# Softmax sums by block transposes from couple 11 on instead of couple 9, half of them moved into the first half of a couple

## The chip, the cores and the metric

The kernel runs on one core of one Trainium2 chip. The metric is the device time of one launch in microseconds (us), the median of some runs. All data are 32-bit floats. The engines are named as the profile names them: PE (matrix products), DVE (vector engine), ACT (activation engine), POOL (GpSimd) and SP (here only a queue of DMAs). PE writes its results to the banks of PSUM, and DVE or ACT must read a bank out (drain it) before PE may fill it again.

## The reference

Attention with normalised queries and keys, and a two-layer network with a SiLU behind it:

```python
# q, k, v: (8 batches, 12 heads, 448 rows, 64); w_in: (768, 2048); w_out: (2048, 768)
rms = np.sqrt(np.mean(x * x, axis=-1, keepdims=True) + 1e-06)     # for x = q and x = k
q_n, k_n = q / rms_q * g_q, k / rms_k * g_k
scores = (1 / np.sqrt(64)) * np.matmul(q_n, k_n.transpose(0, 1, 3, 2))
attn = np.exp(scores - scores.max(-1, keepdims=True))
attn = attn / (attn.sum(-1, keepdims=True) + 1e-09)
x = np.matmul(attn, v)            # then (batch, row, head * 64) -> (3584, 768)
h = x @ w_in
out = (h * (1 / (1 + np.exp(-h)))) @ w_out
```

## The kernel before

**Couples.** The attention is worked off in 24 couples (`c` = 0 to 23), of two pairs of heads each: four heads of one batch. Three couples make a batch, and six (`GROUP`) make two batches, whose network layer is then computed. For a couple, `scores` gives the transposed scores of a block of keys on PE and their exponentials on ACT (L788, with k's norm as ACT's scale), and `weigh` multiplies the exponentials with v on PE (L820, into the banks `av0` and `av1`). `visit(c)` holds these two for couple c, and at its start the end of couple c-1: `divide(c - 1, sums)` (L892) multiplies that couple's result by the inverse softmax sums, which lie in `both_r` (`r[0]` and `r[1]`).

**Between two visits.** `between(c)` runs PE on the first network layer of the last two batches, which is computed by Strassen's seven products (`Seven`): three matmuls of 448 columns each (L992), 14 matmuls in each of the two halves of a `between`. The products go to banks `mm` (two of them) and `sc` (two, which the scores also use). DVE drains most products with an addition (L941), ACT copies some (L1003, L1012) and later applies the SiLU to them (L1145). `fill(others, prompt)` deals other work among these matmuls, in the order in which it is written: `others` evenly over the half, `prompt` one piece at the start and one after each product. What is dealt stands in its engine's queue at that place, and every engine works its queue off in order.

**The other work of a couple.** In the first half: `flip(c + 1, "q")` (L682), `add` (L834), which adds the exponentials of the key blocks up (block 1 in the visit, blocks 2 and the left one, `LEFT`, here), and `normalise(c + 2)`, whose last two pieces are k's sums of squares (ACT squares by L474 into a scratch tile, DVE sums them by L475, POOL takes the root by L503). In the second half, from couple 9 on (`FOLDED = LATE`): `fold(c, i)` twice, which gives the softmax sums over the 128 key rows: DVE transposes 32 x 32 blocks of the added weights into `turned`, a region that holds weights no longer needed (L717), and reduces them (L718). Then `flip(c + 1, "k")` (L686) with ACT's `gain` (L692), and q's squares (L699 on ACT, L705 on DVE). `close(c)` then joins the two halves of rows with small matmuls (L731 for q's norms, L736 for the folded sums) into one `sc` bank, inverts the sums and spreads them by another block transpose (L745, L749, L751); POOL takes q's roots (L743) and scales q (L762).

**Sums on PE.** Couples 6 to 8 get their sums by `sum_up` instead: matmuls of the weights with ones (L861), two reciprocals of 128x224 on DVE (`invert`, L870), a copy (L876) and four DMAs on SP's queue (`spread`, L879), which copy each half of the rows to where the other is. Couple 6 has two such terms (eight matmuls in place of four), because its left block isn't added by DVE.

**Rounding of w_in.** Until couple 10, DVE also rounds and sums w_in (L126, L129, L133; the sums L938 and L941 on `W`).

The order of the instructions on each engine is that in which the program is written; nothing reorders it.

Of the kernel before, what the change touches and what calls it, by code (L numbers as in the profile page):

```python
# [11 lines left out]
F32 = mybir.dt.float32  # L12
# [15 lines left out]
BANK = 512  # L28
# [514 lines left out]
def bounded(  # L543
# [13 lines left out]
    GROUP, LATE = z.NPAIR, z.LATE  # L557
    EARLY = GROUP - 1
    SOON = 2 * GROUP - 1
    FOLDED = LATE  # L560
# [54 lines left out]
    def weights(c, j):  # L615

        return other if j == 0 and c < GROUP and c % 2 else e[j]
# [95 lines left out]

    def fold(c, i):

        turned = weights(c, 1)[:, 1].rearrange("p h s -> p (h s)")
        nc.vector.transpose(turned, weights(c, 0)[:, i].rearrange("p h s -> p (h s)"))  # L717
        nc.vector.tensor_reduce(  # L718
            out=folded[:, ts(i, n)], in_=turned.rearrange("p (n e) -> p n e", e=z.Q),
            axis=AX.X, op=ALU.add,  # L720
        )
# [116 lines left out]
    def sum_up(c):  # L838
# [6 lines left out]
        if c < GROUP:  # L845
            t = bank(S)
        else:
            t = ps.tile([P, 2, BANK], F32, name="sc", bufs=2)[:, 0, 0:S]
# [3 lines left out]
        if c == GROUP:  # L852
            terms.insert(0, (1, None))
# [42 lines left out]
    def normalise(c):  # L896


        def piece(name, i):
            t = scratch[i if c < GROUP + 2 else 0]  # L900
# [612 lines left out]
    def visit(c):  # L1513
# [23 lines left out]
        if c > 0:  # L1537
# [12 lines left out]
            else:  # L1550
                divide(c - 1, sums)
# [46 lines left out]
    def between(c):  # L1598

        def transposes_and_sums():  # L1600
            if c >= FOLDED:
                if c < LATE - 1:
                    transpose_k(c + 1)
                turns = [lambda: flip(c + 1, "k"), gain] if LATE - 1 <= c < NC - 1 else []
                return [lambda: fold(c, 0), lambda: fold(c, 1)] + turns
# [53 lines left out]
        late += further[2:] if c >= GROUP else further[:2]  # L1659
# [10 lines left out]
        if c >= LATE - 2:  # L1670
# [4 lines left out]
            steps = weights_in(c, 1)  # L1675
# [22 lines left out]
    begun, inverting = {}, []  # L1698
# [243 lines left out]
```

## Time and profile before

| | |
|---|---|
| median of three runs | 1295.49 us (1294.70 to 1296.91) |
| the profiled execution | 1295.43 us, its span 1293.6 us |
| PE busy | 1274.9 us, 99% of the span |
| DVE busy | 992.7 us, 77% |
| ACT busy | 504.0 us, 39% |
| POOL busy | 361.2 us, 28% |
| mean granted clock of PE | 0.996 |

The first line is what the launch took from outside, the span is what the instructions take from the first to the last, and the difference of the second row, 1.8 us, lies around the program. Busy time counts an engine's work and not its waiting. The attention takes the span's first 708 us, and the rest is the last network group and the second layer. Times below are us from the span's start; in the timeline a row gives start, length, engine, line, operation, output and inputs, and in brackets how long the engine stood idle before it and for whom. In the table by stretches a row gives the stretch, its length, each engine's busy time with its number of instructions, and PE's granted clock (1.00 is full).

### The profile page before, as it was taken

How to read it: one execution, taken by the hardware profiler on the slowest of the kernel's cores; microseconds unless marked ns; L12 is line 12 of the kernel's file. 1: busy time of each engine (PE TensorE's matmuls, PEld its weight loads, DVE VectorE, ACT ScalarE, POOL GpSimd, SP SyncE). 2: the span in 40 equal slices, each digit the busy share in tenths (PEclk: the TensorE clock that was granted, in tenths of full speed). 3: DMA queues.
4: the chain of work that ended last, by engine and by line, in shares of the span. 5: the costliest groups of instructions: out<-in, count | busy, mean ns of one | idle time of the engine just before them, and what ended most of it. 6: DMA issues, size and time to landing. Idle time of an engine off the chain costs nothing.

```text
span 1293.6 us, 19902 instructions
## 1 busy us (share of the span) xinstructions
PE 1274.9 (99%) x7204; PEld 840.0 (65%) x7204; DVE 992.7 (77%) x1712; ACT 504.0 (39%) x880; POOL 361.2 (28%) x221
## 2 busy tenths in 40 slices
PE   9999999989999999999999999999999999999997
PEld 5444454444554554554544555559999999999997
DVE  6899778868666668766656887798878786868685
ACT  7977576645554554554543444300000000000000
POOL 6756454543344344344311444300000000000000
PEclk9999999989999999999999999999999999999999
DMA  9674447333433433433312466313231414141401
GB/s 237 173 197 128 111 124 195 85 74 86 115 86 86 115 86 86 114 87 86 100 38 86 134 216 205 129 49 91 89 120 60 136 45 148 33 149 40 158 13 40
DMA packets 263280, 140.70 MB, mean 109 GB/s; under 512 B 202788, under 2 KB 247076, under 8 KB 263172
## 3 DMA queue, kind: packets, MB, share of 16 engines
q1 hardware_dynamic: 262544, 138.23, 38.6%
q8 instruction: 59, 0.97, 0.3%
q0 software_dynamic: 320, 0.90, 0.2%
q14 instruction: 49, 0.40, 0.1%
q10 hardware_dynamic: 308, 0.20, 0.1%
HBM read 95.36 MB, written 41.29 MB: 106 GB/s over the span
## 4 chain that ended last, share of the span: by engine, by line
PE 90%; DVE 6%; ACT 2%; issue 1%; SPq 0%; DMA 0%; DVEq 0%; ACTq 0%; POOL 0%; POOLq 0%
PE alone L1314 23%; PE mm L992 17%; PE av L820 10%; PE sc L783 10%; PE sc L992 9%; PE mm L1314 8%; PE alone L992 7%; PE alone L1352 2%; PE mm L861 1%; DVE work L717 1%; PE mm L1352 1%; DVE rms L475 1%; PE sc L674 1%; PE sc L643 1%; ACT stage L1145 1%
## 5 line engine op out<-in xcount | busy, mean ns | idle before, releaser
L788 ACT ACTIVATE work<-sc,rms 128x448 f32<-128x448 f32 x318 | 182.1, 635 | 82.5 <-PE sc L783 70.5
L783 PE MATMUL sc<-work 64*64 64x448 f32 x1344 | 167.8, 543 | 1.4 <-ACT work L653 0.6
L834 DVE TENSOR_TENSOR work<-work 128x896 f32<-128x896 f32 (+1 forms) x112 | 120.5, 1106 | 51.8 <-PE av L820 51.2
L820 PE MATMUL av<-work,rows 64*64 64x448 f32 x1272 | 154.6, 541 | 1.7 <-DVE av L796 1.7
L992 PE MATMUL mm<-x,W 128*128 128x448 f32 x366 | 151.8, 550 | 3.6 <-DVE parts L941 3.6
L992 PE MATMUL mm<-sums_x,W 128*128 128x448 f32 x348 | 141.6, 541 | 1.6 <-DVE stage L941 1.6
L530 POOL DMA_DIRECT2D out_dram<-x x2 | 1.2, 594 | 443.5 <-DVE x L941 443.5
L503 POOL TENSOR_TENSOR rms<-rms,minus_half 128x14 f32<-128x14 f32 (+4 forms) x40 | 96.0, 2403 | 86.4 <-DVE rms L499 82.6
L992 PEld LDWEIGHTS mm<-x,W 128*128 128x128 f32 x366 | 69.5, 193 | 75.6 <-issue 66.5
L1314 PE MATMUL alone<-W,rows 128*128 128x192 f32 x610 | 113.0, 326 | 0.0
L992 PEld LDWEIGHTS mm<-sums_x,W 128*128 128x128 f32 x348 | 65.4, 190 | 68.6 <-issue 62.2
L820 PEld LDWEIGHTS av<-work,rows 64*64 64x64 f32 x1272 | 64.3, 132 | 64.5 <-issue 20.8
L1314 PEld LDWEIGHTS alone<-W,rows 128*128 128x128 f32 x610 | 101.4, 190 | 0.0
L783 PEld LDWEIGHTS sc<-work 64*64 64x64 f32 x1344 | 59.1, 132 | 64.4 <-ACT work L788 25.3
L992 PE MATMUL sc<-x,W 128*128 128x448 f32 x246 | 99.6, 541 | 0.0
L1013 POOL TENSOR_TENSOR stage<-parts,stage 128x448 f32<-128x448 f32 x31 | 39.8, 1283 | 169.5 <-ACT stage L1012 165.8
L743 POOL TENSOR_TENSOR rms<-rms,minus_half 128x28 f32<-128x28 f32 x15 | 72.3, 4822 | 37.7 <-DVE rms L740 37.7
L992 PEld LDWEIGHTS sc<-x,W 128*128 128x128 f32 x246 | 46.4, 190 | 47.0 <-issue 46.7
L1314 PE MATMUL alone<-W,work 128*128 128x192 f32 x382 | 72.2, 326 | 0.0
L1324 ACT COPY rows<-alone 128x192 f32<-128x192 f32 x33 | 10.5, 318 | 141.5 <-PE alone L1314 141.5
L1314 PEld LDWEIGHTS alone<-W,work 128*128 128x128 f32 x382 | 63.8, 190 | 0.0
L1145 ACT ACTIVATE stage<-stage 128x896 f32<-128x896 f32 x63 | 56.8, 944 | 17.1 <-DVE stage L941 16.9
(272 smaller groups left out, 2325.6 us busy)
## 6 DMA issues: line engine op xcount, KB each, us to landing
hidden<-stage SPq DMA_DIRECT2D x63, 448.0 KB, 2.8
work<-hidden SPq DMA_DIRECT2D x21, 1024.0 KB, 5.1
rows<-in_moe_w_out_dram SPq DMA_DIRECT2D x32, 384.0 KB, 3.5
W<-in_moe_w_in_dram SPq DMA_DIRECT2D x22, 512.0 KB, 5.3
x<-hidden SPq DMA_DIRECT2D x7, 1024.0 KB, 5.6
rows<-in_q_dram SPq DMA_DIRECT2D x120, 56.0 KB, 2.2
rows<-in_k_dram SPq DMA_DIRECT2D x120, 56.0 KB, 2.3
rows<-in_k_dram SPq DMA_DIRECT2D x60, 96.0 KB, 2.6
```

Source lines behind the costliest of these rows:

```text
L475: nc.vector.tensor_reduce(out=out, in_=t.rearrange("p (n d) -> p n d", n=n), axis=AX.X, op=ALU.add)
L503: nc.gpsimd.tensor_tensor(out=t, in0=t, in1=half, op=ALU.pow)
L743: nc.gpsimd.tensor_tensor(out=f, in0=f, in1=minus_half.to_broadcast([P, n]), op=ALU.pow)
L783: nc.tensor.matmul(two[ds(half * D, D), h, 0:S], keys[rows, ts(half, D)], qT[rows, pair, :], start=True, stop=True,)
L788: nc.scalar.activation(left_weights(c)[:, h] if j == LEFT else weights(c, j)[:, i, h], two[:, h, 0:S], AF.Exp, scale=norm.column(c, i, h, j),)
L820: nc.tensor.matmul(sums[i][ds(h * D, D), :], v, w, start=(j == 0 and step == 1), stop=(j == LEFT - 1 and step == 1),)
L834: nc.vector.tensor_tensor(out=total, in0=total, in1=more, op=ALU.add)
L992: nc.tensor.matmul(t, self.left(name, s), self.right(name, s), start=s == ends[0], stop=s == ends[1])
L1013: nc.gpsimd.tensor_tensor(out=done[1, 2], in0=u2, in1=p5, op=ALU.add)
L1145: nc.scalar.activation(t, t, AF.Silu)
L1314: nc.tensor.matmul(t, x[:, i], y, start=i == ORDER[0], stop=i == ORDER[-1])
L1352: nc.tensor.matmul(o, a[:, 2 * i + m, t], right_one(name, i)[:, m], start=n == 0, stop=n == len(steps) - 1,)
```

## The change

- Couples 9 and 10 get their softmax sums from `sum_up` (matmuls with ones); `FOLDED` becomes 11. Couple 9 uses four matmuls as couple 8 does, couple 10 eight, as couple 6 does (`FULL`), and DVE no longer adds couple 10's left block.
- Couple 10 is `LAGGED`: its ones matmuls stand at the end of `between(10)` and take an `mm` bank. Its reciprocals and its spread are done in `visit(11)`, one after the first scores, the other after its result has been copied out undivided; `divide` follows in `between(11)`.
- From couple 11 on `fold(c, 0)` stands in the first half, right behind what it needs of the additions, whose order changes for it; `fold(c, 1)` opens the second half.
- From couple 11 on k's squares of couple c + 2 move from the first to the second half, and their scratch is the `turned` region in place of `scratch[0]`. With them go L475's reductions on DVE, the root on POOL and the load of the next k on SP's queue.

```diff
-    FOLDED = LATE
+    FULL = (GROUP, SOON - 1)
+    LAGGED = [SOON - 1]
+    FOLDED = SOON
...
+    def turned(c):
+        return weights(c, 1)[:, 1].rearrange("p h s -> p (h s)")
...
     # sum_up
         if c < GROUP:
             t = bank(S)
+        elif c in LAGGED:
+            t = ps_mm.tile([P, BANK], F32, name="mm")[:, 0:S]
         else:
             t = ps.tile([P, 2, BANK], F32, name="sc", bufs=2)[:, 0, 0:S]
...
-        if c == GROUP:
+        if c in FULL:
             terms.insert(0, (1, None))
...
     # normalise
-            t = scratch[i if c < GROUP + 2 else 0]
+            if c < FOLDED + 2:
+                t = scratch[i if c < GROUP + 2 else 0]
+            else:
+                t = turned(c - 2)[:, i * BANK :]
...
     # visit, after scores(c, 0, 0)
+        if lagging:
+            lagging.pop(0)()
...
     # visit, after weigh(c - 1, LEFT - 1, 1)
-                divide(c - 1, sums)
+                if lagging:
+                    for i in range(2):
+                        nc.vector.tensor_copy(x_of(c - 1, i), sums[i])
+                    lagging.pop(0)()
+                else:
+                    divide(c - 1, sums)
...
     # between: transposes_and_sums
-            if c >= FOLDED:
-                if c < LATE - 1:
-                    transpose_k(c + 1)
-                turns = [lambda: flip(c + 1, "k"), gain] if LATE - 1 <= c < NC - 1 else []
-                return [lambda: fold(c, 0), lambda: fold(c, 1)] + turns
+            if c in LAGGED or c >= FOLDED:
+                turns = [lambda: flip(c + 1, "k"), gain] if c < NC - 1 else []
+                return [lambda: fold(c, 1) if c >= FOLDED else None, lambda: None] + turns
...
     # between: the first half
-        if c > GROUP:
+        if c >= GROUP and c not in FULL:
             late += add(c, LEFT)
         further = normalise(c + 2) if c >= GROUP - 1 else []
+        if c >= FOLDED:
+            late = late[0::2] + late[1:2] + [lambda: fold(c, 0)] + late[3:4]
         late += weights_in(c, 0)
...
-        late += further[2:] if c >= GROUP else further[:2]
+        if c < FOLDED:
+            late += further[2:] if c >= GROUP else further[:2]
+        if c - 1 in LAGGED and c not in LAGGED:
+            late.append(lambda: divide(c - 1, None))
...
     # between: the second half
-            steps = weights_in(c, 1)
+            steps = further[2:] if c >= FOLDED else weights_in(c, 1)
...
+        if c in LAGGED:
+            lagging.extend(next(sum_up(c)))
```

Three places show what moves. In the rows, `sc` and `mm` are banks, `work` the weights and the turned region, `rms` the norms; the changed program's line numbers are higher by 2 to 20.

DVE in the second half of couple 9, before:

```order
L499 TENSOR_SCALAR rms_61<-rms_61 128x14
L717 STREAM_TRANSPOSE work<-work 128x896
L718 TENSOR_REDUCE ones<-work 128x28
L941 TENSOR_TENSOR stage<-mm,parts 128x448
L717 STREAM_TRANSPOSE work<-work 128x896
L718 TENSOR_REDUCE ones<-work 128x28
L126 TENSOR_SCALAR W<-W 128x512
L129 TENSOR_SCALAR W<-W 128x512
L133 SCALAR_TENSOR_TENSOR W<-x_173,W 128x512
L686 STREAM_TRANSPOSE work<-rows 128x896
L941 TENSOR_TENSOR stage<-mm,stage 128x448
```

and the same stretch now:

```order
L499 TENSOR_SCALAR rms_61<-rms_61 128x14
L876 RECIPROCAL work<-sc 128x224
L950 TENSOR_TENSOR stage<-mm,parts 128x448
L876 RECIPROCAL work<-sc 128x224
L882 COPY work<-work 128x448
L126 TENSOR_SCALAR W<-W 128x512
L129 TENSOR_SCALAR W<-W 128x512
L133 SCALAR_TENSOR_TENSOR W<-x_173,W 128x512
L688 STREAM_TRANSPOSE work<-rows 128x896
L950 TENSOR_TENSOR stage<-mm,stage 128x448
```

The folds have given way to two reciprocals and a copy; what follows stands as it stood.

DVE in the second half of couple 10 from the sum for k's norms to the drain of the product that PE's last stall there waits for, before:

```order
L499 TENSOR_SCALAR rms_60<-rms_60 128x14
L717 STREAM_TRANSPOSE work<-work 128x896
L718 TENSOR_REDUCE ones<-work 128x28
L717 STREAM_TRANSPOSE work<-work 128x896
L718 TENSOR_REDUCE ones<-work 128x28
L941 TENSOR_TENSOR stage<-sc,stage 128x448
L938 TENSOR_TENSOR W<-W 128x6x128
L686 STREAM_TRANSPOSE work<-rows 128x896
L941 TENSOR_TENSOR parts<-mm,stage 128x448
```

and now, up to the start of visit 11:

```order
L499 TENSOR_SCALAR rms_60<-rms_60 128x14
L950 TENSOR_TENSOR stage<-sc,stage 128x448
L947 TENSOR_TENSOR W<-W 128x6x128
L688 STREAM_TRANSPOSE work<-rows 128x896
L950 TENSOR_TENSOR parts<-mm,stage 128x448
L947 TENSOR_TENSOR W<-W 128x768
L707 TENSOR_REDUCE rms_60<-rows 128x28
L950 TENSOR_TENSOR parts<-mm,parts 128x448
L744 TENSOR_SCALAR rms_60<-sc 128x28
L876 RECIPROCAL work<-mm 128x224
L800 COPY av_2194<-minus_half 128x1
```

The folds are gone from here, and the first reciprocal stands behind the close, ahead of the small copy (`turn`) for which PE's `weigh` in the visit waits.

ACT in couple 13 from the copy of the first `sc` product on, before:

```order
L1012 COPY stage<-sc 128x448
L474 ACTIVATE rows<-rows 128x512
L474 ACTIVATE rows<-rows 128x384
L699 ACTIVATE rows<-rows 128x896
L1003 COPY stage<-sc 128x448
L1145 ACT_TABLE_LOAD
L1145 ACTIVATE stage<-stage 128x896 x2
L692 ACTIVATE work<-work,gains 128x896
```

and now:

```order
L1021 COPY stage<-sc 128x448
L701 ACTIVATE rows<-rows 128x896
L1012 COPY stage<-sc 128x448
L1154 ACT_TABLE_LOAD
L1154 ACTIVATE stage<-stage 128x896 x2
L474 ACTIVATE work<-rows 128x512
L474 ACTIVATE work<-rows 128x384
L694 ACTIVATE work<-work,gains 128x896
```

k's two squares have moved from ahead of q's to behind the SiLU. DVE's queue in the same half of couple 13, now:

```order
L721 STREAM_TRANSPOSE work<-work 128x896
L722 TENSOR_REDUCE ones<-work 128x28
L475 TENSOR_REDUCE rms_61<-work 128x8
L688 STREAM_TRANSPOSE work<-rows 128x896
L950 TENSOR_TENSOR stage<-mm,stage 128x448
L475 TENSOR_REDUCE rms_61<-work 128x6
L499 TENSOR_SCALAR rms_61<-rms_61 128x14
L707 TENSOR_REDUCE rms_61<-rows 128x28
L950 TENSOR_TENSOR parts<-sc,stage 128x448
```

Here the reduction of k's first squares stands ahead of the turn of k and of both drains; before, it was ahead of the folds, half a couple earlier.

More of the change, by code (lines that the diff above doesn't have):

```diff
@@ L712, in bounded @@
     )
+    def turned(c):
+        return weights(c, 1)[:, 1].rearrange("p h s -> p (h s)")
     def fold(c, i):
-        turned = weights(c, 1)[:, 1].rearrange("p h s -> p (h s)")
-        nc.vector.transpose(turned, weights(c, 0)[:, i].rearrange("p h s -> p (h s)"))
+        nc.vector.transpose(turned(c), weights(c, 0)[:, i].rearrange("p h s -> p (h s)"))
         nc.vector.tensor_reduce(
-            out=folded[:, ts(i, n)], in_=turned.rearrange("p (n e) -> p n e", e=z.Q),
+            out=folded[:, ts(i, n)], in_=turned(c).rearrange("p (n e) -> p n e", e=z.Q),
             axis=AX.X, op=ALU.add,
@@ L1696, in between @@
                 pass
-    begun, inverting = {}, []
+    begun, inverting, lagging = {}, [], []
     load_q(2)
```

## The prediction

> **What bounds the kernel now.** I read the page first, then a table by stretches with one row a couple, then the timeline where that table shows PE standing still.
>
> ```profile
> span 1293.6 us, 19902 instructions
> PE 1274.9 (99%) x7204; PEld 840.0 (65%) x7204; DVE 992.7 (77%) x1712; ACT 504.0 (39%) x880; POOL 361.2 (28%) x221
> PE 90%; DVE 6%; ACT 2%; issue 1%; SPq 0%; DMA 0%; DVEq 0%; ACTq 0%; POOL 0%; POOLq 0%
> ```
>
> PE is the bound: 90% of the chain that ended last, 99% of the span. So a change in DVE's work is worth only what it takes from PE's 1% of waiting, and each matmul it adds is paid in full. By couples (9, 10, 11, 13, 14), with two stretches inside couple 10 behind them:
>
> ```profile
> 210.14:242.94 32.80, 31.23 (x179) 15.69 (x180) 28.51 (x38) 21.30 (x35) 14.23 (x6) 1.00 0.59 160
> 242.94:281.07 38.13, 34.02 (x186) 16.45 (x185) 30.87 (x40) 17.11 (x28) 16.04 (x8) 0.91 0.38 83
> 281.07:312.66 31.59, 31.28 (x189) 15.95 (x186) 21.30 (x30) 16.21 (x25) 12.08 (x6) 1.00 0.33 77
> 345.53:378.00 32.47, 32.47 (x190) 16.43 (x189) 21.37 (x29) 18.21 (x29) 13.77 (x6) 1.00 0.47 116
> 378.00:411.09 33.09, 32.78 (x192) 16.66 (x190) 22.11 (x31) 16.74 (x27) 13.50 (x7) 1.00 0.35 79
> ...
> 271.40:275.20 3.80, 0.17 (x2) 0.09 (x1) 3.80 (x6) 0.61 (x1) 0.00 (x0) 0.78 0.25 101
> 275.20:281.10 5.90, 5.90 (x20) 2.63 (x22) 2.34 (x3) 2.33 (x4) 1.53 (x2) 0.56 0.50 82
> ```
>
> The first column is the length, the second PE's busy time, the fourth DVE's. PE idles 1.57 us in couple 9, 4.11 in couple 10, then 0.31 or nothing. In couple 10 PE is idle for 3.6 us with DVE busy throughout, and then runs at a granted clock of 0.56. DVE is the reason in both couples: 28.51 of 32.80 and 30.87 of 38.13.
>
> **Couple 9.** DVE's second half, then PE's:
>
> ```profile
> 233.08 1.11 DVE L717 STREAM_TRANSPOSE work<-work 128x896 f32<-128x896 f32 x1
> 236.89 1.09 DVE L718 TENSOR_REDUCE ones<-work 128x28 f32<-128x896 f32 x1
> 239.41 1.11 DVE L686 STREAM_TRANSPOSE work<-rows 128x896 f32<-128x896 f32 x1
> 240.44 0.59 DVE L941 TENSOR_TENSOR stage<-mm,stage 128x448 f32<-128x448 f32 x1
> ...
> 234.84 2.42 PE L992 MATMUL mm<-x,W 128*128 128x448 f32 x6
> 241.08 1.77 PE L992 MATMUL mm<-sums_x,W 128*128 128x448 f32 x4 [1.57 <-DVE stage L941]
> ```
>
> PE's product of 234.84 is complete at 237.26, but DVE drains it at 240.44, behind both folds, a rounding and the turn of k; PE needs that bank and waits 1.57 us. Now the prices of what replaces the folds, from the chain of work (24 records of the ones matmuls in early couples) and from the rows of the lines:
>
> ```profile
> 36.69 2.39 PE mm L861 x24
> L870 DVE RECIPROCAL work<-sc x6: 1496/1548/1552, 136.4 to 202.9; 128x224 f32<-128x224 f32 x6
> L876 DVE COPY work<-work x4: 394/395/593, 109.8 to 204.5; 128x448 f32<-128x448 f32 x4
> L879 SPq DMA_DIRECT2D work<-work x14: 540/585/1309, 110.3 to 207.0; - x14
> ```
>
> A matmul leaves two records, so four matmuls are 8 of the 24 records: 2.39 / 3 = 0.8 us of PE, paid in full. DVE's folds, 4 x 1.1 = 4.4 us from 233.08, become 2 x 1.55 + 0.40 = 3.5 us, so the drain falls 0.9 us earlier, ending at 240.1 instead of 241.0, while PE comes to it 0.8 us later, at 240.3 (239.5 + 0.8). I leave 0.2 us for the hand-over. Gain: 1.57 - 0.8 - 0.2 = **0.6 us**. The spread's four DMAs (0.585 us each to issue) stand on SP's queue ahead of saves and loads that are read a visit later, and couple 9's divide too comes only in the visit: nothing.
>
> **Couple 10.**
>
> ```profile
> 259.85 3.02 DVE L834 TENSOR_TENSOR work<-work 64x896 f32<-64x896 f32 x2
> 267.64 1.10 DVE L717 STREAM_TRANSPOSE work<-work 128x896 f32<-128x896 f32 x1
> 272.05 0.61 DVE L941 TENSOR_TENSOR stage<-sc,stage 128x448 f32<-128x448 f32 x1
> 274.48 0.58 DVE L941 TENSOR_TENSOR parts<-mm,stage 128x448 f32<-128x448 f32 x1
> ...
> 246.72 0.98 PE L820 MATMUL av<-work,rows 64*64 64x448 f32 x8 [0.48 <-DVE av L796]
> ...
> 266.82 4.67 PE L992 MATMUL mm<-sums_x,W 128*128 128x448 f32 x12
> 275.12 5.87 PE L992 MATMUL mm<-x,W 128*128 128x448 f32 x8 [3.62 <-DVE parts L941]
> ```
>
> The folds run from 267.64 to 272.05 (4.41 us), and the two additions of the left block took 3.02 with what lies between; both leave. The drain of 272.05 then waits only for its product, which is complete when PE has gone on to the next at 266.82. Behind it stand a sum of w_in (0.9), the turn of k (1.1) and the drain that PE waits for (0.6): its own product is complete at 269.2 (half of the 4.67), it ends near 270.3, and PE asks at 271.5. The stall of 3.62 goes, with 1.2 us to spare.
>
> With it goes the slow clock: the 8 records from 275.12 take 5.87 us, where the 12 before them took 4.67, so 3.1 for eight: 2.8 us lost. The rest of the 4.11 us idle is the 0.48 at 246.72, PE waiting in the visit for DVE's `turn` copy, which stands behind the close of the folded sums; that part of the close leaves as well. Against this stand eight ones matmuls, 1.6 us, and 0.2 us because they take the bank of the last but one product and PE arrives before its drain is through. Gain: 4.11 + 2.8 - 1.6 - 0.2 = **5.1 us**.
>
> On the clock the trace has a stall of 1.57 us that leaves it at 1.00 and one of 3.62 that brings it to 0.56. The Trainium skill, "TensorE: Matmul & The Clock Gate", Part 1, puts the drop at about one idle window of 3.4 us and says that the window runs freely, so that a stall of this length may or may not meet it. By that, executions without the drop exist, and for them this term is 2.3 us; that is a rival below.
>
> The reciprocals of couple 10 move into visit 11, where DVE has room (21.30 busy of 31.59): 3.5 us and two copies in place of two multiplications. The two multiplications come back in the first half. I cost them at nothing; rival 2 has the price if the cover is gone.
>
> **Couples 11 to 21.** The work stays the same but for its place, and so what matters is what DVE is late for. In couples 14, 17, 20 (and 11) it is late at the end:
>
> ```profile
> 398.71 1.79 ACT L1145 ACTIVATE stage<-stage 128x896 f32<-128x896 f32 x2
> 406.81 1.09 DVE L718 TENSOR_REDUCE ones<-work 128x28 f32<-128x896 f32 x1
> 409.35 1.06 DVE L705 TENSOR_REDUCE rms<-rows 128x28 f32<-128x896 f32 x1
> 410.33 0.61 DVE L941 TENSOR_TENSOR stage<-sc,stage 128x448 f32<-128x448 f32 x1
> 316.08 0.98 PE L820 MATMUL av<-work,rows 64*64 64x448 f32 x8 [0.19 <-DVE av L796]
> 410.56 0.24 PE L731 MATMUL sc<-rms,ident 64*64 64x28 f32 x2 [0.20 <-DVE rms L705]
> 411.09 0.98 PE L783 MATMUL sc<-work 64*64 64x448 f32 x8
> ```
>
> The close waits for L705, and the scores of 411.09 for the bank drained at 410.33 to 410.94: couple 14 takes 33.09 where couple 13, with the same matmuls, takes 32.47, so 0.6 us. In the second half one fold (2.2 us) leaves and k's reductions (two of 0.7 at most) come, so L705 falls about 0.8 us earlier or more, and both waits go: 4 x 0.6, less 0.3 because visits 12 and 18, which follow 11 and 17, wait for DVE's `turn` copy as it is (316.08) and would wait for longer: **2.1 us**.
>
> Couples 13, 16 and 19 are the other way about:
>
> ```profile
> 361.09 0.64 ACT L474 ACTIVATE rows<-rows 128x512 f32<-128x512 f32 x1
> 365.78 0.68 DVE L475 TENSOR_REDUCE rms<-rows 128x8 f32<-128x512 f32 x1
> 371.53 1.79 ACT L1145 ACTIVATE stage<-stage 128x896 f32<-128x896 f32 x2
> 373.72 0.59 DVE L941 TENSOR_TENSOR stage<-mm,stage 128x448 f32<-128x448 f32 x1
> 375.21 0.61 DVE L941 TENSOR_TENSOR parts<-sc,stage 128x448 f32<-128x448 f32 x1
> 376.25 1.67 PE L992 MATMUL mm<-x,W 128*128 128x448 f32 x4
> ```
>
> k's first square now stands behind the SiLU, which ends at 373.3; with 0.64 for the square DVE's reduction starts at 374.0 and ends at 374.7. Behind it in DVE's queue: the turn of k (1.1, to 375.8), the drain that was at 373.72 (to 376.3; PE needs the bank at 376.25), k's second reduction, q's (to 378.0), the drain that was at 375.21 (to 378.6). The close at 377.9 and the next scores then wait for DVE, some 0.6 us in all: 3 x 0.6 = **1.8 us lost**. For POOL's root and the next k's load, each half a couple later, the reader is a visit or a couple away: nothing.
>
> **The sum:** 0.6 + 5.1 + 2.1 - 1.8 = 6.0 us. The profiled execution took 1295.43 us, beside a median of 1295.49; 1295.43 - 6.0 = **1289.4 us**. Ends of the unknown terms: couples 13, 16, 19 lose between 0 (no gain, since couple 13 has no idle time now) and 1.5 us each (twice what the last drain ends past the close); couples 11, 14, 17, 20 gain between 0 and 2.4 in all (a loss there is rival 1); couples 9 and 10 gain between 3 and 6.5.
>
> **Rivals.**
>
> 1. Slower: the squares of k hold up DVE in every couple from 11 to 21. A square can start only when the second fold has been reduced, since it writes where that fold was, and DVE waits for it with the turn and two drains behind. For it: couple 13 as worked out. Against it: in couple 14 the SiLU ends at 400.5 and the second fold's reduction (406.81 before) is later than that, so that ACT is free and DVE waits one square, 0.9 us, inside a half that has become 0.8 us lighter. It decides from (5.7 + 2.1) / 11 = 0.7 us a couple on; at 1.0 us the time is 1295.4 - 7.8 + 11 = 1298.6.
> 2. Half the gain: the lagging work brings a new stall at couple 11. Its first reciprocal (1.55) stands ahead of the `turn` copy; PE has 24 records of scores and weighted sums ahead of that wait, 2.4 us by the row of 36.69, so DVE would have to start it 0.8 us late or more. If it costs 1.5 to 2, the time is 1291. The same comes out if the slow clock is not in the timed runs (6.0 - 2.8 = 3.2, so 1292.2); but then the median would lie below the profiled execution, and it doesn't.
> 3. No change: couples 13, 16, 19 lose 1.5 each, couples 11 to 20 gain nothing and a half of couple 10's gain fails: 6.0 - 2.7 - 2.1 = 1.2 at most left, so 1294.2 or more.
>
> **Chances.** 0.2% is 2.6 us, about what a measurement of this kernel can tell from no change (its three runs lie 2.2 apart). The forecast (1287.5 to 1291) has 0.60, a better one without the loss in couples 13, 16, 19 (down to 1286) 0.10, rival 2 0.12, of which 0.08 is under 1292.9, rival 3 0.10, rival 1 0.08. Faster: 0.78; same: 0.14; slower: 0.08. The range 1286.0 to 1294.5 takes in the first three and half of the fourth, and leaves out some 0.15.
>
> **What the profile after would show.** Right: no PE idle over 0.5 us between 200 and 281 and a granted clock of 1.00 there; couple 9 about 32.2 long and couple 10 about 33.0; couple 14 near 32.5 with no wait for L705; couple 13 near 33.1 with DVE waiting for ACT before the reduction of k's squares. Wrong: PE waiting in visit 11 for DVE's copy or in couples 12 to 21 for a drain, or a granted clock under 1 anywhere behind 200.

## The result, and the profile after

| | before | after |
|---|---|---|
| median of the runs | 1295.49 us | 1287.59 us (five runs, 1287.43 to 1289.65) |
| ratio, 95% interval | | 0.9942, 0.9927 to 0.9956 |
| profiled execution, its span | 1295.43, 1293.6 us | 1287.5, 1285.4 us |

The change makes the kernel 7.9 us (0.6%) faster; 1289.4 was forecast. From the page of the changed kernel, the span, the busy times and the chain of work that ended last:

```profile
span 1285.4 us, 19882 instructions
PE 1274.2 (99%) x7212; PEld 838.3 (65%) x7212; DVE 987.3 (77%) x1704; ACT 503.5 (39%) x880; POOL 360.0 (28%) x221
PE 95%; DVE 2%; POOL 1%; issue 0%; ACT 0%; SPq 0%; DMA 0%; DVEq 0%; ACTq 0%; POOLq 0%
```

PE is busy for as long as before, for what it no longer loses to the slow clock (2.7 us) the ones matmuls take (2.3 us); DVE's share of the chain has gone from 6% to 2%. So the time came out of the part of the span in which PE stands idle, 18.7 us before and 11.2 after. The table by stretches, one row a couple, 9 to 15 (stretch, length, PE's busy time, weight loads, DVE, ACT, POOL, granted clock, and behind it the DMA engines' busy share and GB/s):

```profile
210.13:242.04 31.91, 31.91 (x179) 15.69 (x178) 27.55 (x37) 20.05 (x34) 14.21 (x6) 1.00 0.57 153
242.04:274.55 32.51, 32.51 (x188) 16.05 (x187) 22.83 (x31) 18.05 (x29) 17.01 (x8) 1.00 0.51 115
274.55:305.51 30.96, 30.96 (x182) 15.79 (x180) 24.27 (x31) 16.63 (x26) 11.06 (x5) 1.00 0.33 78
305.51:339.19 33.68, 33.17 (x191) 15.90 (x189) 29.84 (x42) 18.15 (x28) 11.78 (x6) 1.00 0.39 88
339.19:372.07 32.88, 32.77 (x192) 16.56 (x190) 21.48 (x30) 17.57 (x29) 11.11 (x5) 1.00 0.39 104
372.07:404.43 32.36, 32.36 (x178) 15.97 (x180) 22.18 (x30) 16.69 (x27) 15.30 (x8) 1.00 0.41 93
404.43:437.18 32.75, 32.74 (x191) 16.36 (x189) 21.96 (x30) 18.14 (x28) 11.80 (x5) 1.00 0.39 88
```

In couples 9, 10, 11 and 14 PE is busy for the whole stretch: their waits are gone, and the clock is full. Couples 12, 13 and 15 have become longer. Over all couples, in us, from the scores that open a couple to those that open the next:

| couple | before | after | difference |
|---|---|---|---|
| 9 | 32.80 | 31.91 | -0.89 |
| 10 | 38.13 | 32.50 | -5.63 |
| 11 | 31.59 | 30.97 | -0.62 |
| 14, 17, 20 | 33.09 to 33.14 | 32.36 to 32.39 | -2.21 together |
| 12, 18 | 32.87, 32.79 | 33.67, 33.31 | +1.32 together |
| 15, 21 | 32.39, 32.36 | 32.75, 32.72 | +0.72 together |
| 13, 16, 19 | 32.45 to 32.47 | 32.86 to 32.88 | +1.23 together |
| 9 to 23 | 497.92 | 491.85 | -6.07 |

So the attention gives 6.07 of the 8.2 us between the two spans. The last matmuls in the timeline of before, and in that of after:

```profile
1284.83 0.49 PE L1314 MATMUL alone<-W,work 128*128 128x192 f32 x2
```

```profile
1278.76 0.49 PE L1323 MATMUL alone<-W,work 128*128 128x192 f32 x2
```

They end at 1285.32 and 1279.25, again 6.07 apart. The other 2.1 us lie behind them: from there to the end of the span it is 8.3 us before and 6.2 after. They are not PE's waiting in the attention, and the last section comes back to them.

In couple 10 the drain that PE had waited for, and PE behind it (DVE, then PE):

```profile
267.88 0.59 DVE L950 TENSOR_TENSOR parts<-mm,stage 128x448 f32<-128x448 f32 x1
...
269.75 3.17 PE L1001 MATMUL mm<-x,W 128*128 128x448 f32 x8
272.88 1.71 PE L867 MATMUL mm<-work,ones 128*32 128x448 f32 x16
```

The drain ends 1.3 us before PE comes to the bank (1.2 were forecast), the eight records take 3.17 us where they took 5.87, and the ones cost 1.64 until the next matmul starts at 274.52.

### The profile page after: what moved, and what is told of

It reads as the page before. It is cut to its first block, busy times and chain, and to the rows that moved or that the text cites. A ratio compares the mean times of both kernels' runs of the same rounds, so it can differ in the third digit from the quotient of the medians.

```text
span 1285.4 us, 19882 instructions
## 1 busy us (share of the span) xinstructions
PE 1274.2 (99%) x7212; PEld 838.3 (65%) x7212; DVE 987.3 (77%) x1704; ACT 503.5 (39%) x880; POOL 360.0 (28%) x221
## 4 chain that ended last, share of the span: by engine, by line
PE 95%; DVE 2%; POOL 1%; issue 0%; ACT 0%; SPq 0%; DMA 0%; DVEq 0%; ACTq 0%; POOLq 0%
PE alone L1323 23%; PE mm L1001 20%; PE sc L1001 10%; PE av L824 10%; PE sc L787 10%; PE mm L1323 8%; PE alone L1001 7%; PE alone L1361 2%; PE mm L867 1%; PE mm L1361 1%; PE sc L645 1%; PE sc L676 0%; DVE work L950 0%; PE sc L867 0%; POOL rms L503 0%
## 5 line engine op out<-in xcount | busy, mean ns | idle before, releaser
L838 DVE TENSOR_TENSOR work<-work 128x896 f32<-128x896 f32 (+1 forms) x110 | 118.0, 1091 | 50.1 <-PE av L824 48.7
L1001 PE MATMUL mm<-x,W 128*128 128x448 f32 x366 | 149.1, 542 | 0.0
```

Of the source, the lines that this page charges most:

```text
L838: nc.vector.tensor_tensor(out=total, in0=total, in1=more, op=ALU.add)
L1001: nc.tensor.matmul(t, self.left(name, s), self.right(name, s), start=s == ends[0], stop=s == ends[1])
```

## The experiments

Every kernel was profiled and timed beside runs of the kernel before on its chip. "Length" is the time from the scores of couple 9 to the end of the attention in the profile, which doesn't depend on when couple 9 starts (that differs by 2 us from profile to profile).

| kernel | median, us | ratio to before, 95% interval | length, us |
|---|---|---|---|
| before (beside e1 to e4, e5 to e8, e9 to e12) | 1295.61, 1295.01, 1294.94 | 1 | 497.92 |
| changed (first time, again) | 1287.59, 1287.67 | 0.9942, 0.9945 (0.9932 to 0.9959) | 491.85, 491.83 |
| e1, sums only | 1287.91 | 0.9943 (0.9931 to 0.9956) | 492.45 |
| e2, moves only | 1294.71 | 0.9996 (0.9987 to 1.0004) | 496.88 |
| e3, fold early, k stays | 1285.56 | 0.9925 (0.9912 to 0.9937) | 489.74 |
| e4, four more matmuls, late operand | 1295.62 | 1.0002 (0.9993 to 1.0012) | 496.77 |
| e5, four more matmuls | 1292.93 | 0.9984 (0.9975 to 0.9993) | 495.30 |
| e6, sums of x behind the copy | 1285.78 | 0.9930 (0.9916 to 0.9943) | 489.54 |
| e7, old scratch | 1287.12 | 0.9940 (0.9925 to 0.9955) | 491.58 |
| e8, no lag | 1287.26 | 0.9941 (0.9926 to 0.9956) | 491.70 |
| e9, division first | 1284.72 | 0.9927 (0.9914 to 0.9941) | 488.88 |
| e10, left block not added | 1293.04 | 0.9986 (0.9977 to 0.9996) | 495.81 |
| e11, four ones | 1283.43 | 0.9916 (0.9903 to 0.9930) | 488.16 |

### The two halves of the change apart

e1 undoes the moves from couple 11 on; what couple 10 leaves to couple 11 stays there:

```diff
-                return [lambda: fold(c, 1) if c >= FOLDED else None, lambda: None] + turns
+                return ([lambda: fold(c, 0), lambda: fold(c, 1)] if c >= FOLDED else [lambda: None] * 2) + turns
...
-            late = late[0::2] + late[1:2] + [lambda: fold(c, 0)] + late[3:4]
...
-            steps = further[2:] if c >= FOLDED else weights_in(c, 1)
+            steps = weights_in(c, 1)
```

> Only the first part of the change: couples 9 and 10 get their sums from matmuls with ones, couple 10's lag, and from couple 11 on folds, additions and k's squares stand where they stood before the change. Theory (couples 9 and 10 bring all of the gain, the moves in couples 11 to 21 cost 0.4 us net): couple 9 is 31.9 long, couple 10 32.5, couples 12 to 21 as before the change, the attention ends at 701.5 us, 0.4 earlier than in the changed kernel, time about 1289. Rival (the moves are needed, without them couple 11 on is late by what couple 10 left over): couples 11 and 12 each longer by 0.5 or more, attention end 702.5 or later.

Couples 9 and 10 are 31.91 and 32.50, and 12 to 21 as before the change. But couple 11 is not (its stretch, then the timeline of DVE and PE at its end):

```profile
274.51:307.20 32.69, 31.30 (x184) 16.02 (x181) 24.20 (x32) 16.20 (x25) 11.58 (x5) 1.00 0.35 81
```

```profile
305.46 1.06 DVE L707 TENSOR_REDUCE rms<-rows 128x28 f32<-128x896 f32 x1
...
306.67 0.24 PE L735 MATMUL sc<-rms,ident 64*64 64x28 f32 x2 [1.28 <-DVE rms L707]
```

Couple 11 is 32.69 long, 1.1 more than before the change: with both folds in its second half DVE comes 1.28 us late to the close, since the reciprocals, copies and divisions of couple 10 now stand in couple 11. DVE is busy for 24.20 us of this couple, where it was for 21.30. So the rival held in couple 11 and the theory in the others, and the attention ends at 702.55, just past the rival's mark of 702.5. In e3 (below), where only the early fold is left of the moves, couple 11 is 30.97: the lag is free because the early fold makes room for it.

e2 is the other half: `FOLDED, MOVED = LATE, SOON`, nothing lags, and the moves are made from `MOVED` on.

> Only the second part: couples 9 and 10 fold as before the change (four block transposes and reductions, nothing lags), and from couple 11 on the first fold stands in the first half and k's squares in the second, in the turned region. Theory: the stall of 3.6 us in couple 10 and the clock of 0.56 behind it stay, couple 10 is 38.1 long; couples 11, 14, 17, 20 are 0.7 shorter, 12, 13, 15, 16, 18, 19, 21 0.3 to 0.8 longer, attention end 708.5 (0.4 later than before the change), time 1295.9. Rival (the prediction's sum: the moves gain 2.1 and lose 1.8, or gain more): attention end 707.8 or earlier.

Couples 11 to 21 changed by -0.64 (11), about -0.74 each (14, 17, 20), +0.36 to +0.52 (12, 15, 18, 21) and +0.41 each (13, 16, 19), +0.14 in all, between the loss of 0.4 of the theory and the gain of 0.3 of the rival. The moves by themselves bring nothing (the interval holds 1). Couple 10 was 36.94 and not 38.1, for the clock was low for a shorter time; that is the next question.

### The slow clock

Four matmuls more (0.78 us each) are put where PE stood still in couple 10. In e4 they repeat the first matmul of the product that PE waits with, in e5 one of a product before it, whose operands are there:

```diff
             t, ends = bank(self.n), (self.steps[0], self.steps[-1])
+            if turns.get("busy") and name == "7":      # busy: second half of couple 10
+                turns["busy"] = False
+                other = ps.tile([P, 2, BANK], F32, name="sc", bufs=2)[:, 1, 0:self.n]
+                for _ in range(4):
+                    s = ends[1]                        # e4: ends[0], and "7" for "5"
+                    nc.tensor.matmul(other, self.left("5", s), self.right("5", s), start=True, stop=True)
```

> The kernel before, with four more matmuls of 128 x 448 (0.78 us each, 3.1 us in all) put where PE stands still for 3.62 us in couple 10; they repeat a product's first matmul into a free bank that nothing reads, so no result changes and DVE's work is the same. Theory (the clock of 0.56 behind that place comes from the idle time): the stall shrinks to about 0.5, the granted clock stays 1.00, couple 10 is 35.3 in place of 38.1, time 1292.7. Rival (the clock falls for another reason, such as what had run before): couple 10 stays 38.1 and the clock below 0.6 behind 275 us, time 1295.5.

> The kernel before with four more matmuls of 128 x 448 at the place where PE stands still for 3.62 us in couple 10; this time they repeat a matmul of the product two before, whose weights lie ready, so that they start when PE would stop. Theory (the slow clock comes from the idle time; it differs from execution to execution): PE's idle time there falls to 0.5 us, the granted clock is 1.00 behind it, couple 10 is 35.3 in every run, the mean clock 0.998 or more in all runs, time 1292.7, the lowest of the kernel before. Rival (the clock falls for another reason): mean clocks of 0.995 to 0.997 as often as before, time 1295.5.

PE's timeline and couple 10's stretch, two fences for e4 and two for e5:

```profile
274.09 3.27 PE L996 MATMUL sc<-x,W 128*128 128x448 f32 x8 [2.09 <-DVE W L938]
```

```profile
243.45:280.46 37.01, 34.44 (x195) 16.89 (x193) 30.86 (x40) 17.11 (x28) 15.74 (x8) 1.00 0.39 85
```

```profile
273.07 3.17 PE L996 MATMUL sc<-sums_x,W 128*128 128x448 f32 x8
276.85 3.27 PE L1000 MATMUL mm<-x,W 128*128 128x448 f32 x8 [0.61 <-DVE parts L941]
```

```profile
244.68:280.21 35.53, 34.44 (x194) 16.88 (x193) 30.85 (x40) 17.11 (x28) 15.74 (x8) 1.00 0.38 85
```

e4 didn't do what it was made for: its matmuls themselves waited for a sum of w_in (L938), 2.09 us, so that the stall changed its place and was not filled. It shows that before the change two waits lay in one, the weights and the bank. The clock stayed full in this profile, but not in every run: in five of the eleven the mean clock is 0.996 or 0.997, below this profile's 0.998, and the time is what it was. In e5 PE idles 0.61 us there, the clock is 1.00 and couple 10 is 35.53 long (35.3 expected). The kernel does 3.1 us more of matmuls and is 2.1 us faster than the kernel before. The mean clock was 0.998 or 0.999 in all eleven runs of e5, and 0.997 or less in 13 of the 15 runs of the kernel before beside them; the one with 0.999 took 1292.48 us. (The mean is under 1 in any case, for it counts a low stretch behind the last matmul too, in the kernel before from 1290.73 us on.) The idle time makes the slow clock.

How long the clock stays low differs from one execution to the next. Short stretches of the kernel before, of e2, and of e10 (below), the granted clock third from the end:

```profile
273.00:274.00 1.00, 0.00 (x0) 0.00 (x0) 1.00 (x2) 0.00 (x0) 0.00 (x0) 0.78 0.00 0
280.00:281.00 1.00, 1.00 (x7) 0.18 (x8) 0.62 (x1) 0.00 (x0) 0.29 (x1) 0.81 0.41 65
```

```profile
275.00:276.00 1.00, 0.00 (x0) 0.00 (x0) 1.00 (x2) 0.26 (x1) 0.00 (x0) 0.87 0.00 0
279.00:280.00 1.00, 1.00 (x3) 0.39 (x3) 0.00 (x0) 0.00 (x0) 0.00 (x0) 0.93 0.34 52
```

```profile
273.90:275.00 1.10, 1.10 (x2) 0.63 (x3) 1.10 (x2) 1.08 (x3) 0.09 (x1) 0.70 0.35 64
277.00:278.00 1.00, 1.00 (x3) 0.38 (x2) 0.00 (x0) 0.00 (x0) 0.00 (x0) 0.62 0.67 107
```

Between the two rows of each pair the clock is 0.50. A mean of 0.78 over 1 us is full speed for 0.56 and half for 0.44; so it falls at 273.56 and, by the 0.81, rises at 280.38: 6.8 us. In e2 it falls at 275.74 and rises at 279.14, 3.4 us; in e10 at 274.34 and 277.76, 3.4. The low clock lasts 3.4 us or twice that, and it starts 2.1, 3.1 and 2.8 us after PE fell idle (at 271.49, 272.65 and 271.50). The Trainium skill, "TensorE: Matmul & The Clock Gate", Part 1, has a free-running window of 3413 ns; these lengths agree with it. Its "after ≥1 idle window (~3.4µs)" does not: in e10 PE was idle for 2.40 us only, and the clock fell 0.44 us after it had started again.

The clock records of the traces show what decides. In each of the 14 profiles the changes of the clock lie whole multiples of 3.4133 us apart (in the kernel before 6.83 us, twice that, and then 1010.35, 296 times), so that windows of this length can be counted from any change. In all 14, a window at full clock in which PE stood idle for 2.06 us or more ends with the fall, and none with 2.00 us or less does. Those that lie nearest to the limit, and couple 9:

| profile | window, us | PE idle in it, us | clock behind it |
|---|---|---|---|
| e10, the stall | 270.92 to 274.34 | 2.40 | 0.50 |
| e4, end of the kernel | 1283.38 to 1286.80 | 2.11 | 0.50 |
| before, the stall | 270.14 to 273.56 | 2.06 | 0.50 |
| before, end of the kernel | 1283.90 to 1287.31 | 2.00 | 1.00 |
| before, couple 9 | 239.42 to 242.84 | 1.57 | 1.00 |
| e4, the stall | 269.62 to 273.04, 273.04 to 276.45 | 1.04, 1.05 | 1.00 |

So e4's 2.09 us left the clock alone because they lay by halves in two windows, and the same stall costs the clock in one execution and not in the next, by where it falls. This is read from the traces; no run was made to test it, and PE's ends in them are modelled.

### What made couple 10 late

e8 keeps the ones and takes the lag away (`LAGGED = []`): reciprocals and copy stand again in couple 10's second half. e10 is the kernel before without `add(10, LEFT)`.

> The changed kernel, but couple 10 gets its sums as couple 9 does: its eight ones matmuls open the second half, the reciprocals and the spread stand there and the division in visit 11. Theory (what matters is how long DVE is held ahead of the drains): the reciprocals and the copy, 3.5 us in place of 4.4 of folds, are still ahead of the drains; PE comes 1.6 later, so a stall of about 1.1 is left, too short to lose the clock: couple 10 is 33.6 to 33.9 in place of 32.5, time 1288.9. Rival (the ones alone take the stall away and the lag is not needed): couple 10 is 32.5 or less, time 1287.5.

> The kernel before with one thing left out: DVE does not add couple 10's left block to the weights (two additions of 64 x 896, 3.0 us with the time between them), so couple 10's softmax sums lack that block. Folds stay. Theory (couple 10 was late by what DVE held in the whole couple, not by the folds alone): the stall shrinks from 3.62 to between 0.6 and 2.3 (DVE may wait for the squares of k in between), the clock stays 1.00, couple 10 is 32.3 to 34.1 in place of 38.1, mean clock 0.998 or more. Rival (the folds alone make the stall, as the prediction's account of the drains reads): the stall stays over 3.0 and couple 10 over 36.5.

e8, DVE and PE:

```profile
265.18 2.97 DVE L876 RECIPROCAL work<-sc 128x224 f32<-128x224 f32 x2
268.18 0.39 DVE L882 COPY work<-work 128x448 f32<-128x448 f32 x1
...
270.92 0.58 DVE L950 TENSOR_TENSOR parts<-mm,stage 128x448 f32<-128x448 f32 x1
...
271.91 3.17 PE L1001 MATMUL mm<-x,W 128*128 128x448 f32 x8
```

The rival won: no stall, couple 10 is 32.66 long, and the lag is worth 0.16 us there and nothing in the time. e10, PE and the stretch:

```profile
273.90 4.97 PE L992 MATMUL mm<-x,W 128*128 128x448 f32 x8 [2.40 <-DVE parts L941]
```

```profile
242.95:278.96 36.01, 33.12 (x187) 16.09 (x185) 28.04 (x38) 17.01 (x28) 15.77 (x8) 0.95 0.40 87
```

The two additions are worth 1.2 us of the stall, not 3.0, for DVE then waits 1.7 us for other things in the meantime (0.71 for a product, 0.99 for a square of k); and 2.40 us of idle time, 0.1 over the range that I had expected, still lose the clock, where I had expected it to stay. Against the kernel before, counted from the start of couple 10, the drain of 270.92 comes 3.0 us earlier in e8 (28.55 in place of 31.54): 1.2 from the additions, 4.4 - 3.3 = 1.1 from folds to reciprocals, and 0.7 from visit 10, which is shorter without the close of couple 9's folds. The last helps nothing against the stall, for it brings PE forward too: PE, 1.6 later by its ones, asks for the bank only 1.0 later in all (29.54 in place of 28.55). So 1.2 and 1.1 on DVE and 1.6 on PE, 3.9 together, ended the stall of 3.62; by these figures no one or two of them would have.

### What the moves cost in couples 12 to 21

e3 leaves the early fold and puts k's squares, sums, root and load back into the first half, with their old scratch. e7 leaves them in the second half but gives them the old scratch; q's squares use part of the same memory, so its norms of k from couple 13 on are not the reference's.

```diff
-            if c < FOLDED + 2:
-                t = scratch[i if c < GROUP + 2 else 0]
-            else:
-                t = turned(c - 2)[:, i * BANK :]
+            t = scratch[i if c < GROUP + 2 else 0]      # e3 and e7
...
-        if c < FOLDED:                                  # e3 alone
-            late += further[2:] if c >= GROUP else further[:2]
+        late += further[2:] if c >= GROUP else further[:2]
...
-            steps = further[2:] if c >= FOLDED else weights_in(c, 1)
+            steps = weights_in(c, 1)                    # e3 alone
```

> The changed kernel, but k's squares, their sums, the root on POOL and the load of the next k stay in the first half as before the change, with the scratch of before; the first fold stands in the first half as in the changed kernel. Theory (the loss in couples 13, 16, 19 is ACT's SiLU ahead of k's squares, the loss in 12 and 18 POOL's root ahead of the addition there): 13, 16, 19 are 32.45 again, 12 and 18 near 32.8, couples 14, 17, 20 keep 32.4, attention end about 699.5, time 1287. Rival (the early fold makes DVE late in the first half, where k's sums still stand): couples 12 to 21 each longer by 0.3 to 0.5, attention end 703 or later.

> The changed kernel with one difference: k's squares, in the second half as in the changed kernel, are written to the scratch of before in place of the turned region, so that they need not wait for the second fold. Theory (the place behind the SiLU and ahead of the drains costs, not the region): couples 13, 16, 19 stay at 32.9, couples 15 and 21 at 32.7, time within 1 us of 1287.6. Rival (the squares wait for the fold's reduction): couples 13, 16, 19 fall to 32.5 or below, time 1286.3.

Stretches of couples 12, 13 and 15 in e3, then of 13 and 15 in e7:

```profile
307.60:340.82 33.22, 32.74 (x190) 16.00 (x189) 29.71 (x42) 18.28 (x28) 11.41 (x5) 1.00 0.41 90
340.82:373.30 32.48, 32.48 (x191) 16.45 (x189) 21.27 (x29) 17.32 (x28) 13.64 (x6) 1.00 0.44 112
...
405.74:438.21 32.47, 32.47 (x190) 16.44 (x189) 21.90 (x30) 18.18 (x28) 11.36 (x5) 1.00 0.44 98
```

```profile
338.90:371.79 32.89, 32.78 (x193) 16.59 (x190) 21.48 (x30) 17.64 (x29) 11.12 (x5) 1.00 0.38 102
404.15:436.90 32.75, 32.74 (x190) 16.37 (x189) 21.86 (x30) 18.30 (x28) 12.20 (x5) 1.00 0.39 88
```

The place of k's squares costs, and not their region: e7 is as long as the changed kernel, and in e3 couples 13, 16 and 19 have their 32.45 back, 15 and 21 are within 0.1 of before, while 14, 17 and 20 keep their gain but for 0.1. e3 is 2.1 us shorter than the changed kernel. But couples 12 and 18 (33.22 and 33.14) missed the 32.8 of my theory, which had blamed POOL's root. The wait in visit 12, in the changed kernel (with the drain that POOL holds up there) and in e3:

```profile
305.80 0.62 DVE L950 TENSOR_TENSOR stage<-mm,parts 128x448 f32<-128x448 f32 x1 [1.75 <-POOL stage L1025]
...
309.47 0.98 PE L824 MATMUL av<-work,rows 64*64 64x448 f32 x8 [0.50 <-DVE av L800]
```

```profile
311.38 0.98 PE L824 MATMUL av<-work,rows 64*64 64x448 f32 x8 [0.48 <-DVE av L800]
```

It is much the same without the root: counted from the start of couple 12, e3's drain starts at 0.11 where the changed kernel's starts at 0.29. In e7 and e8 the root stands in the second half too, but POOL is through 0.07 and 0.29 us before the couple starts; there the drain starts at 0.01 and couple 12 is 33.39 and 33.38 long. So POOL's lateness costs 0.3 us in couple 12 of the changed kernel, and nothing in couple 18, where the drain starts at 0.01 too. For the rest DVE is late there by its own queue: PE arrives earlier, and a drain, two sums of x, the close and the `turn` copy stand in a row. e6 and e9 tried that.

The loss of couples 15 and 21, and of the second halves of 12 and 18, is another. In couple 15 of the changed kernel, and in that of e3:

```profile
428.64 0.61 DVE L950 TENSOR_TENSOR parts<-mm,parts 128x448 f32<-128x448 f32 x1
429.31 0.30 PEld L1001 LDWEIGHTS mm<-sums_x,W 128*128 128x128 f32 x2 [0.73 <-DVE parts L950]
```

```profile
430.38 0.61 DVE L947 TENSOR_TENSOR parts<-mm,parts 128x448 f32<-128x448 f32 x1
430.45 2.42 PE L998 MATMUL mm<-sums_x,W 128*128 128x448 f32 x6
```

In the changed kernel the product waits for the drain and starts 0.17 us late; in e3 it starts while the same drain is under way. The semaphores in the traces tell them apart: with k's squares in the second half (changed, e2, e7, e8, e12) this product waits for DVE's semaphore and the next but one, on `mm` again, for ACT's; with them in the first half (before, e1, e3, e6, e9, e11) it waits for ACT's, which the copy L1021 (L1012 before) has long raised, and the later one for DVE's. So the two `mm` banks are taken in the other order, in all four couples. Why the place of k's work changes that order no run shows.

### Two steps further

Both start from e3. e6 moves the two sums behind the `turn` copy; e9 moves all twelve sums of visits 12 and 18 behind the division too:

```diff
     # between, at the end of a group
-            elif c < NC - 1:
-                sum_x([c // GROUP * 2, c // GROUP * 2 + 1], 0, range(2))
     # visit, behind turn
-                sum_x(last_two(c), 0, range(2, 4))
+                sum_x(last_two(c), 0)                # e6; e9 has no such line
     # visit, behind divide (e9)
-                    for i in range(1, HW):
+                    for i in range(HW):
```

> The third experiment's kernel (first fold early, k's squares where they stood), and the two sums of x at the end of couples 11 and 17 (1.2 us of DVE ahead of the close) are done in visits 12 and 18 behind the small copy that PE waits for there. Theory (these visits wait because the drain, two sums, the close and the copy follow one another on DVE, not because of POOL): the wait of 0.65 goes, couple 12 is 32.6 and couple 18 32.5 long, time 0.6 x 2 = 1.2 less than 1285.6, 1284.4. Rival (POOL's addition or the drain behind it sets the copy): couples 12 and 18 stay at 33.2 and 33.1, time 1285.6.

> As the kernel with the two sums of x behind the turn copy, but all twelve sums stand behind visit 12's (and 18's) division too, which empties the banks that PE fills next. Theory (PE's wait moved from the copy to the division, since both stand in one queue of DVE behind the sums): no wait over 0.1 us is left in the visits 12 and 18 but for ACT's exponentials, couples 12 and 18 are 32.5 long, time about 1.1 less than the third experiment's kernel in the same attention, 488.6 from the start of couple 9 to the end of the attention (489.7 there). Rival (the sums come late for a later reader): couples 12 and 18 stay above 33.0.

The division in visit 12 on DVE's timeline and couple 12's stretch, two fences for e6 and two for e9:

```profile
312.38 1.15 DVE L898 TENSOR_TENSOR x<-av,work 128x448 f32<-128x448 f32 x2
```

```profile
307.42:340.52 33.10, 33.05 (x190) 16.07 (x188) 29.56 (x42) 18.28 (x28) 11.35 (x5) 1.00 0.41 90
```

```profile
310.22 1.16 DVE L898 TENSOR_TENSOR x<-av,work 128x448 f32<-128x448 f32 x2 [1.34 <-PE av L824]
```

```profile
306.09:338.86 32.77, 32.77 (x191) 16.31 (x189) 29.84 (x42) 16.46 (x28) 11.36 (x5) 1.00 0.38 85
```

In e6 the wait at the copy is gone, as the theory has it, but couple 12 is only 0.1 shorter: the division came no earlier, and PE's next weighing waits for the banks it empties. With the division first it starts 4.13 us into the couple in place of 4.96, the visit (from the start of its first scores matmul to that of its last) is 10.66 long (11.36 in e3), and couples 12 and 18 are 32.77 each. That is 0.3 more than the theory had: the third product behind the visit starts 0.14 and 0.22 us late. Its sums are not to blame, for they are through 2.3 us before it. Its bank is freed by the visit's last exponentials; ACT stands idle for 4.49 us before these (2.23 in e3) and waits for DVE's additions L838, which now stand behind the twelve sums.

e11 adds to e9 that couple 10 takes four ones matmuls and DVE its left additions back: `FULL = (GROUP,)`.

> As the kernel with the division first, but couple 10 uses four ones matmuls, and DVE adds its left block in the first half as before the change. Theory (PE had 1.2 us to spare at the place of the former stall, and DVE's second half is light): couple 10 falls by the four matmuls, 0.8, or by less if a short stall comes, 31.7 to 32.3, time 0.5 less than the kernel with the division first. Rival (3.0 us of additions bring the stall back): couple 10 over 33.0.

```profile
242.07:273.83 31.76, 31.76 (x180) 15.79 (x179) 25.55 (x33) 18.14 (x29) 16.78 (x8) 1.00 0.50 114
```

Couple 10 falls by the 0.75 us of four matmuls, and PE still waits for nothing there. e11 is the fastest kernel of all, 1283.43 us; it is 1.3 us faster than e9, where its attention is 0.7 shorter and 0.5 was expected. The changed kernel, once more on the same chip, took 1287.67:

> The changed kernel once more, on the same chip and beside the same runs as the other three of this call, to compare them with it: 1287.6, couples 13, 16, 19 at 32.9, couples 12 and 18 at 33.3 to 33.7.

It had couples 13, 16 and 19 at 32.85 to 32.88, and 12 and 18 at 33.67 and 33.31 (in e7 and e8 couple 12 was 33.4).

## Why the prediction was right, step by step

The time lay in the range, and the attention gave 6.07 us where the sum had 6.0. That agreement is partly luck: couples 9 and 10 gave 0.8 more than their terms, the moves 0.7 less than theirs, and 2 us came from where nothing was forecast.

- **Couple 9**, 0.6 forecast, 0.89 measured. The stall of 1.57 went as worked out, and PE's busy time rose by 0.68, not by 0.8. The 0.2 for the hand-over was not paid.
- **Couple 10**, 5.1 forecast, 5.63 measured: 3.62 of stall, 2.70 of slow clock (5.87 to 3.17) and 0.68 in the visit (11.28 to 10.60; the term was 0.48) against 1.64 for the ones with their hand-over (1.8 forecast); the other 0.3 is the restart of the matmuls behind the stall and the close, which no longer joins folded sums. That both folds and additions leave was right, and so was the room of 1.2 us. That the lag belongs to the gain was not said, and e8 shows that it doesn't.
- **The slow clock** as a term was right (e5). Rival 2 set executions without it aside because the median doesn't lie below the profiled execution. That holds for most runs and not for all: some lack it, by their mean clock of 0.999, such as that of 1292.48 us. It is in most, with one or two windows' length, so the median holds most of it.
- **The reciprocals in visit 11 at nothing**: right in the changed kernel, but the cover is the early fold. Without the moves couple 11 pays 1.1 us (e1): a stall of the kind of rival 2, though at the close and not at the copy, and smaller than its 1.5 to 2.
- **Couples 11, 14, 17, 20**, 2.4 forecast before the visits behind them, 2.83 measured, by the mechanism named: the fold leaves the second half, and no wait for L705 (now L707) is left.
- **Visits 12 and 18**, 0.3 taken off for the two. The mechanism was right, the size was not: PE comes earlier to a copy that DVE can't bring forward, and visit 12 became 0.53 us longer (0.24 without POOL's lateness, e7), visit 18 0.25. The whole loss in couples 12 and 18 was 1.3.
- **Couples 13, 16, 19**, 0.6 each forecast, 0.41 measured, by the chain worked out. In couple 13:

```profile
367.53 0.69 DVE L475 TENSOR_REDUCE rms<-work 128x8 f32<-128x512 f32 x1 [1.97 <-ACT work L474]
...
371.31 0.61 DVE L950 TENSOR_TENSOR parts<-sc,stage 128x448 f32<-128x448 f32 x1
```

  DVE waits for the square behind the SiLU; counted from the couple's start the reduction comes at 28.34 (28.5 forecast) and the last drain at 32.12 (32.5).
- **Couples 12, 15, 18, 21 and their second half**: this is the step that failed. They were given no term, and lose 0.27 us each in their second half, at a product that starts 0.17 late (0.28 by its second matmul). With k's squares in the first half the loss is gone (e3), so their place is the cause. The wait is that for the drain behind the second fold, whose bank the product takes in the changed kernel and not in e3; why it takes another bank stays open.
- **POOL's root at nothing**: it cost 0.3 us, in couple 12 alone (e7, e8).
- **Rival 1** (every couple from 11 on slower) had its mechanism, DVE waiting for the square behind the SiLU, in couples 13, 16 and 19, and other losses in four more; they came to 3.27 us over the eleven couples, 0.3 each, where it decides from 0.7 on.
- **Rival 3's sum** (1.2 us left) leaves out the half of couple 10's gain that its own condition takes away, 2.6 more; forecast and range don't use it.

## What to carry to other kernels

A stall of the bounding engine is the sum of what its partner does ahead of it in a whole stage: here (e8) 1.2 and 1.1 us less on DVE and 1.6 us more on PE, its ones, ended a stall of 3.62 together, and the ones were worth their 1.6 us because the slow clock went with the stall. Before a partner's work is moved, ask for each moved piece what it must wait for in its new place (k's squares behind the SiLU), and what else moves with it: the early fold alone was worth 2 us more than the early fold with k's squares moved out of its way. A wait that is taken away at one reader shows at the next (the copy, then the division), so the reader's whole chain has to be moved.

## What the runs showed of the hardware

Filling a stall with matmuls whose result nobody reads made the kernel faster by 2.1 us (e5), since the low clock lasts 3.4 or 6.8 us. A stall need not be as long as that: in the 14 profiles the clock fell at the end of each window of 3.4133 us in which PE was idle for 2.06 us or more, and of none with 2.00 us or less. A stall of 2.09 us that lay across two windows (e4) left it at 1.00, and one of 2.40 us within a window (e10) did not.

The 2 us at the end: from the last matmul to the end of the span it is 8.2 to 8.4 us in all five profiles of kernels that fold in couples 9 and 10 (before, e2, e4, e5, e10), and 6.0 to 7.0 in all nine that use ones there. In the former the fourth of SP's closing semaphore instructions starts 2.1 to 2.3 us behind the third, in the latter at once. SP issues eight DMAs more in the latter (the spreads of two couples). By the trace of the kernel before, the two semaphores that the late one waits for had been raised by 1286.65, and it starts at 1292.22; so it isn't these transfers. Why the end is shorter no run here shows; it is a part of the gain that belongs to no wait on PE.
